# Attention and mixer on one core: f loaded by two broadcast transfers, one weight load on ScalarE's queue, the Exp table loaded early, new opening orders

## The chip, the cores and the metric

The kernel runs on one core of a Trainium2 chip. The metric is the device time of one execution in microseconds. Of three timed executions of the kernel before, the median is 926.94 us (926.46 to 927.48). One further execution was profiled; it took 927.18 us, and its span, from the first to the last instruction, is 925.4 us. Two kernels of this program count as different when their times differ by more than 0.2%, some 1.85 us.

## The reference

```python
# attention: 8 batches, 8 heads, 576 positions, head size 64; f is [8, 8, 576]
scores = scale * np.matmul(q, k.transpose(0, 1, 3, 2))
log_f = np.log(np.clip(f, 0.0001, 1.0))
cum = np.cumsum(log_f, axis=-1)
decay = cum[:, :, :, None] - cum[:, :, None, :]
scores = np.where(causal, -1000000000.0, scores + decay)
attn = np.exp(scores - max); attn = attn / (sum + 1e-09)
out = np.matmul(attn, v)
# mixer on x [8, 576, 512]
h = np.maximum(xt @ w_tok1, 0.0) @ w_tok2
u = x + h.transpose(0, 2, 1)
h2 = np.maximum(u @ w_ch1, 0.0) @ w_ch2
return u + h2
```

The four weight matrices arrive as 64-bit floats, two 32-bit words each, and the kernel decodes them itself.

## The kernel before

**Opening.** The 64 rows of f (one row per batch and head, 576 values of 4 bytes) are laid twice into a tile `xt` by four transfers of 32 rows, two on SP's queue and two on ScalarE's (`ld` in `decay`, L517). VectorE clips (L525), ScalarE takes the logarithm (L526), VectorE sums along the row (L528) and makes `cd` (L531, L533), ScalarE writes a copy times -8 (L536), and two transfers store that to DRAM as `decd` (L538), from where each pair of heads reads its decay `cb` (L732).

**Pairs of heads.** There are 32 pairs (n0, n1, ...). For each one `raw` holds q and k (L719), `vr` holds v. TensorE makes scores into eight banks (L747), for some pairs, n0 among them, it adds the decay by matmuls with `cd` (L774), for the others VectorE adds `cb`. VectorE reduces the minimum and frees the bank (L788), ScalarE takes the exponential (L792), TensorE transposes (L862), ScalarE or VectorE copy that out (L872, L870), TensorE multiplies by v (L891). While TensorE has nothing to do at the start, 36 small filling matmuls of the identity run (L545).

**Decoding.** `decode` loads a block of weights into one of three buffers `d_raw` (L559), and ScalarE (L572), VectorE (L576, L580, L584, L592) and GpSimd (L588, L492, L495) turn it into two 32-bit parts. The first five blocks belong to w_tok1; the first is loaded by two transfers, the second by one of 256 KB.

**Mixer.** After every four pairs the token mixer of half a batch runs; from about 380 us on the channel mixer of the whole output runs, nearly all of it matmuls.

**What sets the order.** `ORDER` is a table of numbers with one list for each engine and one for SP's queue: the operations in the order in which that engine issues them. Each engine issues strictly in that order, so an instruction that waits holds back all that stand behind it. For SP's queue there is also a pace: a transfer is issued only when an older one has landed, so that no more than about 1.2 MB stand between the two (`AHEAD`).

Of the kernel before, what the change touches and what calls it, by code (L numbers as in the profile page):

```python
# [67 lines left out]
    ),  # L68
    DVE=(
# [369 lines left out]
def build(nc, env, dims):  # L439
# [39 lines left out]
    def at(b):  # L479
        return env[b.kind][b.slot]  # L480
# [28 lines left out]
    def decay():  # L509
# [6 lines left out]
        def ld(eng, q):  # L516
            return eng.dma_start(at(w)[32 * q : 32 * q + 32, 0, :], fs[q // 2])  # L517

        p.op("POOL", 600, lambda: nc.gpsimd.memset(row(2), 0.0), wr=["zero"], bufs=[w, *HOLD.values()])
        for q in (0, 2):  # L520
            dma(lambda q=q: ld(nc.sync, q), 73728, wr=[("f", q)], bufs=[w])
# [1015 lines left out]
```

## Time and profile before

| | before |
|---|---|
| median of three runs | 926.94 us |
| profiled execution | 927.18 us, span 925.4 us |
| PE (TensorE) busy | 905.5 us, 98% |
| DVE (VectorE) busy | 710.2 us, 77% |
| ACT (ScalarE) busy | 520.6 us, 56% |
| POOL (GpSimd) busy | 237.2 us, 26% |
| DMA | 242.49 MB, mean 262 GB/s |

PE is the engine with the largest share, over the whole span. The shares are means over stages that differ: the first 20 us hold the opening, up to 380 us the pairs of heads and the token mixer run, then the channel mixer. SP, the queue that issues nearly all transfers, has no busy time of its own in these shares.

### The profile page before, as it was taken

What the parts mean: (1) busy time and instruction counts of PE and PEld (TensorE: products, weight loads), DVE (VectorE), ACT (ScalarE), POOL (GpSimd) and SP (SyncE); (2) the same over time, 40 slices, a digit from 0 to 9 for tenths busy, and PEclk for the clock granted to TensorE, in tenths of its full rate; (3) what the DMA queues carried; (4) which work ended last, traced back from release to release, by engine and by line L of the source; (5) the groups of instructions that cost most, each with busy time, mean ns of one, the idle gap of its engine ahead of it and who ended that gap; (6) DMA issues with size and microseconds to landing.
All of it is one profiled execution on the core that took longest, in us unless ns stands there. A gap on an engine that the chain in (4) does not pass through costs nothing.

```text
span 925.4 us, 26760 instructions
## 1 busy us (share of the span) xinstructions
PE 905.5 (98%) x10270; PEld 781.3 (84%) x10270; DVE 710.2 (77%) x1894; ACT 520.6 (56%) x1340; POOL 237.2 (26%) x320
## 2 busy tenths in 40 slices
PE   7999999999998999999999999999999999999998
PEld 5688888788887787888888888888888899999998
DVE  7998988888777777754699646986389955995497
ACT  5989998998788988731354123541135412542142
POOL 4577776766665562110000000000000000000000
PEclk9999999999999999999999999999999999999999
DMA  7999999998999698558887878888888799889986
GB/s 237 273 268 281 312 280 292 302 282 274 276 304 285 207 271 224 167 176 293 263 257 234 265 208 245 250 252 261 261 244 247 239 294 303 286 273 298 294 286 220
DMA packets 143871, 242.49 MB, mean 262 GB/s; under 512 B 15936, under 2 KB 71488, under 8 KB 143744
## 3 DMA queue, kind: packets, MB, share of 16 engines
q1 hardware_dynamic: 143648, 240.64, 84.8%
q8 instruction: 81, 1.33, 0.6%
q14 instruction: 46, 0.38, 0.1%
q10 hardware_dynamic: 96, 0.15, 0.0%
HBM read 199.52 MB, written 41.21 MB: 260 GB/s over the span
## 4 chain that ended last, share of the span: by engine, by line
PE 59%; DVE 2%; DMA 2%; POOL 1%; issue 0%; ACT 0%; SPq 0%; DVEq 0%; POOLq 0%
PE bank L1047 9%; PE bank L1049 9%; PE bank L1048 9%; PE bank L1128 9%; PE bank L1130 9%; PE bank L1129 9%; PE bank L1245 2%; DMA d_raw<-ud 1%; DVE pr L788 1%; PE bank L891 1%; PE bank L862 0%; DMA wq<-wd 0%; DMA recd<-rs 0%; POOL sg L495 0%; PE bank L747 0%
## 5 line engine op out<-in xcount | busy, mean ns | idle before, releaser
L792 ACT ACTIVATE pr<-pr,nmin 64x64 f32<-64x64 f32 (+4 forms) x320 | 176.7, 560 | 16.6 <-DVE nmin L788 16.2
L489 ACT ACTIVATE st<-H 128x512 fp32r<-128x512 f32 (+1 forms) x210 | 119.6, 586 | 89.0 <-PE bank L1129 63.3
L1128 PE MATMUL bank<-st,wq 128*128 128x512 f32 (+1 forms) x420 | 154.2, 367 | 0.3 <-DMA wq<-wd 0.3
L1130 PE MATMUL bank<-st,wq 128*128 128x512 f32 (+1 forms) x420 | 154.3, 367 | 0.0
L1129 PE MATMUL bank<-st,wq 128*128 128x512 f32 (+1 forms) x420 | 154.2, 367 | 0.0
L788 DVE CUSTOM_DVE_ANT_0 pr<-bank,cb 128x448 f32<-128x448 f32 (+3 forms) x260 | 108.7, 454 | 6.0 <-PE bank L747 1.8
L747 PE MATMUL bank<-raw 64*64 64x448 f32 (+6 forms) x1408 | 109.5, 397 | 2.6 <-DMA raw<-in_qk 1.3
L498 DVE TENSOR_TENSOR st<-H,st 128x512 fp32r<-128x512 f32 (+1 forms) x150 | 92.4, 631 | 14.6 <-ACT st L489 14.2
L891 PE MATMUL bank<-pf,vr 64*64 64x256 f32 (+3 forms) x2048 | 98.7, 317 | 1.5 <-ACT pf L872 0.5
L983 DVE TENSOR_TENSOR tmp<-bank,tmp 128x512 f32<-128x512 f32 (+1 forms) x80 | 50.2, 632 | 55.6 <-PE bank L1049 42.4
L872 ACT ACTIVATE pf<-bank 128x512 f32<-128x512 f32 x152 | 84.4, 596 | 11.2 <-PE bank L862 5.7
L1128 PEld LDWEIGHTS bank<-st,wq 128*128 128x128 f32 x420 | 78.8, 188 | 10.2 <-issue 0.6
L1130 PEld LDWEIGHTS bank<-st,wq 128*128 128x128 f32 x420 | 78.8, 188 | 9.9
L1129 PEld LDWEIGHTS bank<-st,wq 128*128 128x128 f32 x420 | 78.8, 188 | 9.6
L891 PEld LDWEIGHTS bank<-pf,vr 64*64 64x64 f32 x2048 | 76.4, 134 | 10.0 <-issue 2.0
L747 PEld LDWEIGHTS bank<-raw 64*64 64x64 f32 x1408 | 52.0, 132 | 27.7 <-issue 10.2
L1073 ACT ACTIVATE H<-bank 128x512 f32<-128x512 f32 (+1 forms) x30 | 16.5, 554 | 103.2 <-PE bank L1049 103.1
L1059 ACT ACTIVATE tmp<-bank 128x512 f32<-128x512 f32 (+1 forms) x30 | 16.6, 552 | 101.1 <-PE bank L1049 101.1
L862 PE MATMUL bank<-ident,pr 64*128 64x64 f32 x1536 | 65.0, 225 | 5.4 <-issue 2.1
L862 PEld LDWEIGHTS bank<-ident,pr 64*128 64x128 f32 x1536 | 58.8, 139 | 11.2 <-issue 5.0
L922 POOL TENSOR_TENSOR xt<-xt,rb 128x64 f32<-128x64 f32 (+1 forms) x64 | 52.5, 840 | 49.7 <-DVE xt L910 19.6
L792 ACT ACTIVATION_READ_ACCUMULATOR pr<-pr,nmin 128x1 f32 (+1 forms) x320 | 63.2, 198 | 0.0
(171 smaller groups left out, 2109.9 us busy)
## 6 DMA issues: line engine op xcount, KB each, us to landing
wq<-wd SPq DMA_DIRECT2D x420, 256.0 KB
raw<-in_qk SPq DMA_DIRECT2D x32, 576.0 KB
cb<-decd SPq DMA_DIRECT2D x26, 576.0 KB
d_raw<-in_w_ch SPq DMA_DIRECT2D x48, 256.0 KB
wd<-sg SPq DMA_DIRECT2D x24, 512.0 KB
vr<-in_v SPq DMA_DIRECT2D x64, 160.0 KB
rb<-recd SPq DMA_DIRECT2D x32, 320.0 KB
wd<-sg SPq DMA_DIRECT2D x24, 384.0 KB
```

The lines of the kernel that those rows point to most:

```text
L489: nc.scalar.activation(out, in_, func, scale=scale)
L498: nc.vector.tensor_tensor(out, in_, asf(hi), op=ALU.subtract)
L747: nc.tensor.matmul(at(buf)[HALF[h], of : of + n], q[:, i0 : i0 + D], k[:, j0 : j0 + n], start=t not in (0, 1), stop=not nd, skip_group_che ...
L788: nc.vector.tensor_tensor_reduce(o, x, y, -1.0 / D**0.5, c0[:m, NS + z : NS + z + 1] if t == 5 else 3e38, op0=ALU.add, op1=ALU.min, accum_ ...
L792: nc.scalar.activation(x, x, AF.Exp, bias=E["nmin"][sm][:m, t : t + 1], scale=-1.0, accum_out=E["rec"][rm][:m, c : c + 1])
L862: nc.tensor.transpose(at(ps[s])[:, k * D : (k + 1) * D], at(pr)[r, x, :, :].rearrange("p a b -> p (a b)"), E["ident"][r, r])
L872: p.op("ACT", d_act(512), lambda src_=src_, o=o: nc.scalar.activation(o(), src_(), AF.Copy), rd=[ps[s]], wr=[(pt, s)], bufs=[ps[s], pt])
L891: nc.tensor.matmul(at(av[z])[o, 256 - w : 256], at(vr)[r, vblk(j), :], at(pt)[r, c : c + w], start=j == 4, stop=gi == 2, skip_group_check= ...
L1047: nc.tensor.matmul(o, wt[:, 0, :], h_, start=(first and k == 0), stop=False, skip_group_check=True)
L1128: nc.tensor.matmul(o, wt[:, 0, :], h_, start=(first and x == 0), stop=False, skip_group_check=True)
L1129: nc.tensor.matmul(o, wt[:, 1, :], h_, start=False, stop=False, skip_group_check=True)
L1130: nc.tensor.matmul(o, wt[:, 0, :], l_, start=False, stop=(x == FX - 1), skip_group_check=True)
```

## The change

f comes by two transfers of 64 rows, one on each queue, each of which reads its 32 rows of f twice through a source that is broadcast over a leading count of two. The transfer of the second decoding's weights moves from SP's queue to ScalarE's, where it stands behind the first table load. A one-column Exp is put ahead of the copy times -8, so that the Exp table is loaded there and not at the first exponential. The orders of all engines are new in the opening and the first batches; from about the tenth pair of heads on they are the old ones, with numbers that are lower by two.

```diff
-        "14:12 145 135 146 136 26:2 139 155 28:3 156 140 185 31:11 193 202 42:3 188 45:4 165 49 168 171 267 275 218 284 "
...
+        "12:21 143 137 144 133 33 134 153 34:3 138 37:2 183 154 39 186 191 40 200 41:3 163 44:2 166 169 46 265 47 273 "
...
-        def ld(eng, q):
-            return eng.dma_start(at(w)[32 * q : 32 * q + 32, 0, :], fs[q // 2])
+        def ld(eng, s):
+            return eng.dma_start(at(w)[D * s : D * s + D, 0, :], fs[s : s + 1].to_broadcast([2, HB // 2, S]))
+
+        def neg():
+            nc.scalar.activation(E["lnx"], E["lnx"], AF.Exp)
+            return nc.scalar.activation(row(0), row(1), AF.Copy, scale=-8.0)
...
-        for q in (0, 2):
-            dma(lambda q=q: ld(nc.sync, q), 73728, wr=[("f", q)], bufs=[w])
-        for q in (1, 3):
-            p.op("ACT", 450, lambda q=q: ld(nc.scalar, q), wr=[("f", q)], bufs=[w], lat=2300, at=-1.0)
+        dma(lambda: ld(nc.sync, 0), 147456, wr=[("f", 0)], bufs=[w])
+        p.op("ACT", 450, lambda: ld(nc.scalar, 1), wr=[("f", 1)], bufs=[w], lat=2300, at=-1.0)
...
-        p.op("ACT", d_act(S, False), lambda: nc.scalar.activation(row(0), row(1), AF.Copy, scale=-8.0), rd=["c"], wr=["f"], bufs=[w])
+        p.op("ACT", d_act(S, False), neg, rd=["c"], wr=["f"], bufs=[w])
...
-            return nc.sync.dma_start(o, src.bitcast(U32).rearrange("... (n two) -> ... n two", two=2))
+            return (nc.scalar if tok == ("t1", 1) else nc.sync).dma_start(o, src.bitcast(U32).rearrange("... (n two) -> ... n two", two=2))
...
-            dma(lambda x=x: ld(*x), nb / len(loads), wr=[(rb, i)], bufs=[rb])
+            if tok == ("t1", 1):
+                p.op("ACT", 450, lambda x=x: ld(*x), wr=[(rb, i)], bufs=[rb], lat=4000, at=-1.0)
+            else:
+                dma(lambda x=x: ld(*x), nb / len(loads), wr=[(rb, i)], bufs=[rb])
```

SP's queue from its first transfer on, before (raw_183 is q and k of n0, raw_184 of n1; d_raw_150 holds the first decoding's weights, d_raw_151 the second's):

```order
L517 DMA xt_144<-in_f 32x576 x2
L719 DMA raw_183<-in_qk 128x1152
L559 DMA d_raw_150<-in_w_tok 64x512 x2
L559 DMA d_raw_151<-in_w_tok 128x512
L719 DMA raw_184<-in_qk 128x1152
L559 DMA d_raw_152<-in_w_tok 128x512
L538 DMA decd<-xt_144 32x576 x2
```

The same stretch of the change:

```order
L516 DMA xt_144<-in_f 64x1x576
L723 DMA raw_183<-in_qk 128x1152
L560 DMA d_raw_150<-in_w_tok 64x512 x2
L723 DMA raw_184<-in_qk 128x1152
L560 DMA d_raw_152<-in_w_tok 128x512
L539 DMA decd<-xt_144 32x576 x2
```

One transfer of f stands ahead of n0's q and k where two stood, and the second decoding's weights are gone from the queue.

ScalarE's instructions from its first transfer on, before:

```order
L517 DMA xt_144<-in_f 32x576 x2
L524 ACT_TABLE_LOAD
L524 ACTIVATE lnx<-rec_95 128x1
L526 ACTIVATE xt_144<-xt_144 128x576
L536 ACTIVATE xt_144<-xt_144 128x576
L572 ACTIVATE d_g_153<-d_raw_150 128x256
L572 ACTIVATE d_g_154<-d_raw_151 128x256
L572 ACTIVATE d_g_153<-d_raw_152 128x256
L792 ACT_TABLE_LOAD
L792 ACTIVATE pr_193,rec_92<-pr_193,nmin_89 64x64
```

The same stretch of the change:

```order
L516 DMA xt_144<-in_f 64x1x576
L525 ACT_TABLE_LOAD
L525 ACTIVATE lnx<-rec_95 128x1
L560 DMA d_raw_151<-in_w_tok 128x512
L527 ACTIVATE xt_144<-xt_144 128x576
L519 ACT_TABLE_LOAD
L519 ACTIVATE lnx<-lnx 128x1
L520 ACTIVATE xt_144<-xt_144 128x576
L576 ACTIVATE d_g_153<-d_raw_150 128x256
L576 ACTIVATE d_g_154<-d_raw_151 128x256
L576 ACTIVATE d_g_153<-d_raw_152 128x256
L796 ACTIVATE pr_193,rec_92<-pr_193,nmin_89 128x7x64
```

The second table load has moved from ahead of the first exponential to behind the logarithm, and a transfer stands between the first one-column activation and the logarithm.

VectorE's instructions from the clip on (idb and tri are small constants), before:

```order
L525 TENSOR_SCALAR xt_144<-xt_144 128x576
L1399 TENSOR_SCALAR idb<-ident 64x64 x2
L1400 TENSOR_SCALAR tri<-mask 64x64 x2
L528 SCALAR_TENSOR_TENSOR xt_144<-xt_144 128x576
L531 TENSOR_SCALAR cd<-xt_144 128x576
L533 SCALAR_TENSOR_TENSOR cd<-cd,lows,xt_144 128x576
L576 TENSOR_SCALAR d_g_153<-d_g_153 128x256
L580 TENSOR_SCALAR d_g_153<-d_g_153 128x256
L584 SCALAR_TENSOR_TENSOR d_g_153<-d_raw_150,d_g_153 128x256
L576 TENSOR_SCALAR d_g_154<-d_g_154 128x256
L788 ISA pr_193,nmin_89<-bank_64,mask 64x64
```

The same stretch of the change:

```order
L526 TENSOR_SCALAR xt_144<-xt_144 128x576
L1403 TENSOR_SCALAR idb<-ident 64x64 x2
L1404 TENSOR_SCALAR tri<-mask 64x64 x2
L529 SCALAR_TENSOR_TENSOR xt_144<-xt_144 128x576
L532 TENSOR_SCALAR cd<-xt_144 128x576
L534 SCALAR_TENSOR_TENSOR cd<-cd,lows,xt_144 128x576
L580 TENSOR_SCALAR d_g_153<-d_g_153 128x256
L584 TENSOR_SCALAR d_g_153<-d_g_153 128x256
L580 TENSOR_SCALAR d_g_154<-d_g_154 128x256
L588 SCALAR_TENSOR_TENSOR d_g_153<-d_raw_150,d_g_153 128x256
L584 TENSOR_SCALAR d_g_154<-d_g_154 128x256
L792 ISA pr_193,nmin_88<-bank_63,mask 128x7x64
```

All that works on f still stands ahead of the decoding and of the first reduction; one more decoding instruction now stands ahead of that reduction, which is another one. On TensorE, 21 filling matmuls stand ahead of n0's first scores where 12 stood.

## Rows read from the trace of the kernel before

**Rows 1.** Busy time of each engine by stage; last three columns: clock, DMA share, GB/s.
```profile
core 0: us, PE busy (x) PEld busy (x) DVE busy (x) ACT busy (x) POOL busy (x), PEclk, DMA share, GB/s
8.00:20.00 12.00, 11.09 (x164) 7.09 (x164) 10.38 (x44) 7.52 (x22) 6.12 (x10) 1.00 0.79 250
20.00:40.00 20.00, 17.46 (x367) 12.54 (x367) 20.00 (x86) 18.69 (x60) 9.81 (x15) 1.00 0.88 262
40.00:70.00 30.00, 28.92 (x580) 23.80 (x580) 28.62 (x100) 26.61 (x77) 22.59 (x29) 1.00 0.98 279
70.00:160.00 90.00, 89.76 (x1873) 77.09 (x1864) 79.29 (x293) 81.21 (x245) 67.16 (x88) 1.00 0.95 289
```

**Rows 2.** Timeline of the opening: start, us, engine, line, what, [idle before <-releaser].
```profile
0.74 0.87 SPq L517 DMA_DIRECT2D xt<-in_f  x2
...
3.94 0.46 DVE L525 TENSOR_SCALAR xt<-xt 128x576 f32<-128x576 f32 x1 [2.41 <-DMA xt<-in_f]
...
4.22 2.50 PE L545 MATMUL bank<-ident 128*64 128x48 f32 x22
...
7.10 0.82 DVE L533 SCALAR_TENSOR_TENSOR cd<-cd,lows,xt 128x576 fp32r<-128x576 f32 x1
...
8.00 1.85 PE L747 MATMUL bank<-raw 64*64 64x448 f32 x20 [1.28 <-DMA raw<-in_qk]
...
8.57 0.79 SPq L538 DMA_DIRECT2D decd<-xt  x2
...
8.97 0.80 ACT L572 ACTIVATE d_g<-d_raw 128x256 f32<-128x256 f32 x2 [1.68 <-DMA d_raw<-in_w_tok]
...
9.43 0.29 DVE L576 TENSOR_SCALAR d_g<-d_g 128x256 uint32<-128x256 uint32 x1 [1.51 <-ACT d_g L572]
...
10.09 0.43 DVE L584 SCALAR_TENSOR_TENSOR d_g<-d_raw,d_g 128x256 f32<-128x256 uint32 x1
...
13.71 1.28 ACT L792 ACT_TABLE_LOAD   x1
...
15.00 0.35 ACT L792 ACTIVATE pr<-pr,nmin 64x64 f32<-64x64 f32 x1
```

**Rows 3.** DMA view of the window 1.75 to 3.25 us: packets, MB, share.
```profile
DMA packets 210, 0.38 MB, mean 252 GB/s; under 512 B 64, under 2 KB 64, under 8 KB 210
...
q10 hardware_dynamic: 96, 0.15, 27.0%
```

**Rows 4.** DMA view of the whole span: packets, queue, issues by form with KB each.
```profile
DMA packets 143871, 242.49 MB, mean 262 GB/s; under 512 B 15936, under 2 KB 71488, under 8 KB 143744
...
q1 hardware_dynamic: 143648, 240.64, 84.8%
...
wq<-wd SPq DMA_DIRECT2D x420, 256.0 KB
...
recd<-rs SPq DMA_DIRECT2D x32, 5.0 KB
...
d_raw<-ud SPq DMA_DIRECT2D x4, 32.0 KB
xt<-ud SPq DMA_DIRECT2D x4, 32.0 KB
...
```

**Rows 5.** Three short windows around the transfers of f; columns as in Rows 1.
```profile
1.50:1.75 0.25, 0.00 (x0) 0.00 (x0) 0.03 (x1) 0.09 (x1) 0.25 (x2) 1.00 0.00 0
1.75:3.25 1.50, 1.41 (x4) 0.79 (x4) 0.00 (x0) 1.40 (x2) 1.14 (x7) 1.00 1.00 252
8.00:10.00 2.00, 2.00 (x22) 0.85 (x24) 0.53 (x2) 0.80 (x2) 0.00 (x0) 1.00 0.94 335
```

**Rows 6.** Timeline of TensorE near 289 us, after its longest idle stretch past the opening.
```profile
289.29 0.89 PE L862 MATMUL bank<-ident,pr 64*128 64x64 f32 x19 [2.12 <-issue]
```

**Rows 7.** The two windows that follow it; columns as in Rows 1.
```profile
290.00:292.00 2.00, 2.00 (x38) 1.88 (x38) 0.79 (x2) 2.00 (x5) 2.00 (x3) 0.50 0.65 222
292.00:294.00 2.00, 2.00 (x50) 1.91 (x46) 1.29 (x2) 2.00 (x8) 1.20 (x2) 0.70 1.04 339
```

More of the change, by code (lines that the diff above doesn't have):

```diff
@@ L514, in row @@
             return at(w)[:, i, :]
-        def ld(eng, q):
-            return eng.dma_start(at(w)[32 * q : 32 * q + 32, 0, :], fs[q // 2])
+        def ld(eng, s):
[3 more added lines that the diff above has]
+            return nc.scalar.activation(row(0), row(1), AF.Copy, scale=-8.0)
         p.op("POOL", 600, lambda: nc.gpsimd.memset(row(2), 0.0), wr=["zero"], bufs=[w, *HOLD.values()])
-        for q in (0, 2):
-            dma(lambda q=q: ld(nc.sync, q), 73728, wr=[("f", q)], bufs=[w])
-        for q in (1, 3):
-            p.op("ACT", 450, lambda q=q: ld(nc.scalar, q), wr=[("f", q)], bufs=[w], lat=2300, at=-1.0)
+        dma(lambda: ld(nc.sync, 0), 147456, wr=[("f", 0)], bufs=[w])
+        p.op("ACT", 450, lambda: ld(nc.scalar, 1), wr=[("f", 1)], bufs=[w], lat=2300, at=-1.0)
         p.op("ACT", 1500, lambda: nc.scalar.activation(E["lnx"], E["rec"][3][:, :1], AF.Ln), wr=["ln"], at=-1.0)
-        p.op("DVE", d_dve(S, True), lambda: nc.vector.tensor_scalar(row(0), row(0), 1e-4, 1.0, op0=ALU.max, op1=ALU.min), rd=[("f", q) for q in range(4)], wr=["f"], bufs=[w], port=True)
+        p.op("DVE", d_dve(S, True), lambda: nc.vector.tensor_scalar(row(0), row(0), 1e-4, 1.0, op0=ALU.max, op1=ALU.min), rd=[("f", q) for q in range(2)], wr=["f"], bufs=[w], port=True)
         p.op("ACT", d_act(S, False), lambda: nc.scalar.activation(row(0), row(0), AF.Ln), rd=["ln"], wr=["f"], bufs=[w])
```

397 rows, old and new, of tables (ACT, DVE, PE, POOL) are left out of this document.

## The prediction

> **What bounds the kernel now.** I read the stages first. From 20 to 40 us VectorE has no idle time at all (20.00 of 20.00 us) while TensorE lacks 2.5 us; from 40 to 70 both are nearly full; from 70 to 160 TensorE works 89.76 of 90 us and VectorE 79 [rows 1]. So the opening is VectorE's, and what VectorE loses there TensorE has lost when its own full stretch begins: nothing later gives it back. The question is then when VectorE becomes busy for good. The timeline says 9.43 us [rows 2]: the 1.51 us of idle time ahead of that end with ScalarE's first decoding step, which itself waited 1.68 us for the first decoding's weights, until 8.97. Ahead of it VectorE worked on f: the clip starts at 3.94, when f has landed, and cd is done at 7.10 + 0.82 = 7.92. f is thus 9.43 - 7.92 = 1.5 us early now, and no more. TensorE's first scores start at 8.00, when n0's q and k land; they aren't what VectorE waits for, since it has decoding to do until 10.6.
>
> The profiled execution takes 927.18 us for a span of 925.4; it lies 0.24 us above the median, and I forecast the median.
>
> **Two transfers of f, not four.** What goes away is one issue on SP and one on ScalarE, 0.87 / 2 = 0.43 us each [rows 2]. The bytes stay: 64 rows of 2304 bytes, twice, 295 kB. What may change is how many of the 16 DMA engines carry them. In the window in which f moves, 64 packets are under 512 bytes, and no row of f is that small: 16 for each of the four transfers. ScalarE's queue shows 96 packets for its two, and 96 = 2 x (32 rows + 16) [rows 3]. So a transfer ends with one small packet from each engine that it used, and a transfer of 32 rows used 16. It isn't always 16. The list holds 902 transfers on SP's queue (first line x420, the small ones x32, x4 and x4). With 16 small packets each these would be 14432; the 32 stores of `recd` add 32 x 20 rows of 256 bytes = 640, the eight 32 KB loads 8 x 128 = 1024 more, in all 16096. The page counts 15936 [rows 4]. With 10 engines for each `recd` store, whose outermost count is 20, the sum is 16096 - 32 x 6 = 15904, and 32 are left for the instruction queues. So the transfer is cut evenly along its outermost count: 32, 64 and 128 give 16, and 20 gives 10.
>
> The changed transfer writes 64 rows, but its source now begins with a count of two. If both sides have to be cut, it can only be cut in two. No row of before shows a transfer whose two sides differ in this way, so both ends stay open: 16 engines, or two. I take two, since a cut that only one side can follow is of no use to the other, and all other rows follow the outermost count.
>
> The Trainium skill says it outright (DMA: Bandwidth & Descriptors, Why a DMA increments its semaphore by 16 and not by 1): the engines used are the largest number up to 16 that divides the slowest dimension of both sides, and they are the lowest-numbered ones, so that both transfers of f would share the same two. The 32 stores with 10 engines agree with its first half. No run here shows the second yet.
>
> The cost. On two engines, the same two for both queues (that is assumed; separate pairs are a rival), each engine carries 295 / 2 = 147.5 kB. Over the whole span a busy engine moves 240.64 MB / (0.848 x 16 x 925.4 us) = 19.2 kB per us [rows 4]. While f moves it is 252 / 16 = 15.8, and from 8 to 10 us 335 / (0.94 x 16) = 22.3 [rows 5]. So f takes 7.7 us (6.6 to 9.3). Nothing moves ahead of 1.75 us, all small packets are through by 3.25, and the clip starts 0.69 later [rows 2, 3, 5]. f lands at 1.75 + 7.7 + 0.69 = 10.1 (9.0 to 11.8), not at 3.94. Clip to cd takes 7.92 - 3.94 = 3.98, and all of it stands ahead of the decoding in VectorE's order, so decoding starts at 14.1 (13.0 to 15.8) in place of 9.43. That is **+4.7 us** (+3.6 to +6.3).
>
> What is late next: q and k of n0 and the first weights stand behind f on these two engines. Their shares there are 590 / 16 = 36.9 and 262 / 16 = 16.4 kB, with the second weights 16.4 more, together 217 kB: 1.75 + 11.3 + 0.69 = 13.7, still ahead of 14.1. But the same arithmetic for before gives 1.75 + 71.7 / 19.2 + 0.69 = 6.2, and the weights came at 8.97, so up to 2.8 more, 16.5, and with 0.46 for ScalarE's step VectorE would start at 17.0, +7.5. TensorE's filling matmuls, 21 now, end near 4.22 + 20 x 2.50 / 11 = 8.8; then it idles some 4 us. After a pause of 2.12 us its granted clock was 0.50 for 2 us, the lower level (1.2 GHz), and 0.70 over the next two [rows 6, 7]. At half pace the first scores cost up to 1.6 us more, and the decoding ahead of the first reduction, four steps of 0.29 and one of 0.43, hides part of that. I add **0.5 us** (0 to 1.6) for both.
>
> **The other parts.** The second weights' issue on ScalarE, about 0.45 us, ends before the logarithm can start, now as before. On their own queue these 262 kB can take turns with n0's q and k, which were ahead of them: at worst 16.4 / 19.2 = 0.85 us later for all that lands; at best SP's queue is 0.43 earlier. I take **0**, as f hides either. The table load of 1.28 us ahead of the first exponential at 15.00 goes; behind the logarithm it lies beside the scan on VectorE (about as long) and delays at most the store of `decd`, now at 8.57. The gain stays on ScalarE, while VectorE is the bound: **0**, at best -1.0 if TensorE's transposes were waiting on that exponential alone. If f had been on time, the cover of this load would be the same scan. The new orders issue the same operations, and VectorE has no idle time in 20 to 40 us to win back: **0**, -1 to +1 for TensorE's 1.1 us of gaps from 40 to 70.
>
> The sum: 927.18 + 4.7 + 0.5 = 932.4, as a median 932.1; I forecast **932.1 us**. Its own range goes from +2.6 (3.6 - 1.0) to +8.5 (7.5 + 1.0): 929.5 to 935.4.
>
> **The rivals.** (a) f runs on 16 engines, as now. Then f stays early, decoding starts when the first weights land, between 0.43 earlier and 0.85 later: 926.5 to 927.8, no change. For it: the tile side has 64 rows. Against it: the stores with 10. (b) Two engines for each transfer, but not the same two: 73.7 kB each, 3.8 us, f at 6.3, cd at 10.3, +0.8: 927.7, no change. It decides where f lands before some 5.5 us; later than that, each us counts in full. (c) f on 16 engines, and what ScalarE gains passes, or the pause of 2.12 us with its slow clock [rows 6, 7] (2.12 + 2 x 0.5 + 2 x 0.3 = 3.7 us in all) doesn't return, as it hangs on instants that any new order moves: from 923.2 up to the bound of a difference at 925.1, faster. Nothing in the rows says that it goes. (d) The second weights hold n0's q and k back beside a prompt f; this is the 0.85 of (a) and not slower by itself.
>
> The Trainium skill has a rule for (d) (DMA: Bandwidth & Descriptors, Queues, rings and completion order): each DMA engine takes turns between the queues that have work for it. By that rule the upper end of (a), 927.8, would be the likelier one; no row of before shows two full queues at once for long.
>
> **How the numbers follow.** Two engines and the same two: 0.74. Of that 0.03 ends within 0.2% (1.85 us), with the fastest rate and the gains of the other parts. (a) 0.14, (b) 0.05, (c) 0.07. So faster 0.07, within 0.2% 0.22, slower 0.71. Without (a) and (b) the range would hold 7 in 10 at most, so it takes them in: 926.4 to 935.4.
>
> **What would show it.** After the change the clip starts near 10 us, waiting for f, and VectorE idles until then; the DMA share between 2 and 8 us falls; ScalarE's queue shows 64 + 2 + 128 + 16 = 210 packets, against 224 on 16 engines; the first exponential comes near 19 to 20 us. The prediction is wrong if the clip starts near 4 us, and its size is wrong if f lands as here and VectorE's loss is then made up before 70 us, where the rows show no room for it.

## The result, and the profile after

The changed kernel takes 937.24 us (median of 6 runs, 933.97 to 939.86), the kernel before 926.75 us beside it: ratio 1.0109, with an interval of 1.0085 to 1.0133, so 7.9 to 12.3 us more. I had forecast 932.1, in a range up to 935.4. The profiled execution took 937.34 us for a span of 935.5.

First the opening, in the timeline of the changed kernel (start, length, engine, line, what, idle before it), as in [rows 2]:

```profile
0.74 1.13 ACTq L516 DMA_DIRECT2D xt<-in_f  x1
0.74 0.72 SPq L516 DMA_DIRECT2D xt<-in_f  x1
...
12.84 0.46 DVE L526 TENSOR_SCALAR xt<-xt 128x576 f32<-128x576 f32 x1 [11.31 <-DMA xt<-in_f]
...
14.18 2.41 PE L751 MATMUL bank<-raw 64*64 64x448 f32 x20 [6.80 <-DMA raw<-in_qk]
...
16.00 0.82 DVE L534 SCALAR_TENSOR_TENSOR cd<-cd,lows,xt 128x576 fp32r<-128x576 f32 x1
...
16.74 0.29 DVE L580 TENSOR_SCALAR d_g<-d_g 128x256 uint32<-128x256 uint32 x1
...
20.55 0.62 DVE L792 CUSTOM_DVE_ANT_0 pr<-bank,mask 128x448 f32<-128x448 f32 x1 [1.05 <-PE bank L778]
...
21.76 0.67 ACT L796 ACTIVATE pr<-pr,nmin 128x448 f32<-128x448 f32 x1 [0.72 <-DVE nmin L792]
```

The clip waits for f until 12.84 us, not 3.94. VectorE's decoding follows cd at 16.74, 7.3 us later than before, and ScalarE's first exponential comes at 21.76, not at 15.00. Then there is a wait that the kernel before did not have: VectorE's reduction at 20.55 waits for a bank that TensorE fills with the falling term (L778).

The windows answer to [rows 1], columns as there (the last three: granted clock, DMA share, GB/s):

```profile
8.00:20.00 12.00, 5.44 (x36) 2.36 (x36) 6.40 (x19) 3.48 (x6) 1.39 (x3) 0.54 0.43 117
20.00:40.00 20.00, 18.48 (x256) 11.72 (x256) 16.64 (x72) 14.85 (x49) 8.89 (x14) 0.76 0.69 232
40.00:70.00 30.00, 27.97 (x596) 22.03 (x595) 29.76 (x113) 26.18 (x79) 18.68 (x25) 1.00 0.87 270
70.00:160.00 90.00, 89.24 (x1854) 76.32 (x1846) 80.24 (x291) 82.04 (x245) 69.51 (x88) 1.00 0.95 286
10.00:12.00 2.00, 0.00 (x0) 0.00 (x0) 0.00 (x0) 0.00 (x0) 0.00 (x0) 0.50 0.13 49
```

VectorE is busy 6.40 us from 8 to 20 (10.38 before) and 16.64 of 20 after that, where it had no idle time before. In the last row no engine computes, and the DMA moves 49 GB/s. VectorE's waits in the first 45 us (total, times, longest):

```profile
DVE xt L526 <- DMA xt<-in_f: 11.3, 1, 11.3
DVE pr L792 <- PE bank L778: 3.6, 3, 1.4
```

The DMA view, of the window 1.75 to 3.25 us as in [rows 3], then of the whole span as in [rows 4]:

```profile
DMA packets 21, 0.07 MB, mean 49 GB/s; under 512 B 0, under 2 KB 0, under 8 KB 21
```
```profile
DMA packets 143811, 242.49 MB, mean 259 GB/s; under 512 B 15876, under 2 KB 71428, under 8 KB 143684
...
q10 hardware_dynamic: 210, 0.41, 0.2%
```

21 packets where 210 went before: a few engines work. ScalarE's queue counts 210 packets, and the small ones fall by 60, from 4 x 16 to 2 x 2.

How far the loss travels is seen from the 16 stores of `ud` on SP's queue (the token mixer's u of half a batch, each), the first, the tenth and the eleventh, of the kernel before and then of the changed one:

```profile
80.29 0.59 SPq L1331 DMA_DIRECT2D ud<-xt  x1
...
291.24 1.01 SPq L1331 DMA_DIRECT2D ud<-xt  x1
315.06 0.32 SPq L1331 DMA_DIRECT2D ud<-xt  x1
```
```profile
90.45 0.59 SPq L1335 DMA_DIRECT2D ud<-xt  x1
...
302.60 0.61 SPq L1335 DMA_DIRECT2D ud<-xt  x1
324.16 0.32 SPq L1335 DMA_DIRECT2D ud<-xt  x1
```

10.2 us are lost by the first store, of which 7.3 are the later start of the decoding, and 11.4 by the tenth; 2.3 come back by the eleventh; the span is 10.1 longer. TensorE's pause of 2.12 us near 289 us [rows 6] has no counterpart in the changed kernel. That the 2.3 are this pause is not shown: it lies ahead of the tenth store, and the return shows only behind it. So a loss as large as the whole one stands at the first store, but it is not simply carried from there to the end (more on this below).

### The profile page after: what moved, and what is told of

It reads as the page before. It is cut to its first block, busy times and chain, and to the rows that moved or that the text cites. A ratio compares the mean times of both kernels' runs of the same rounds, so it can differ in the third digit from the quotient of the medians.

```text
span 935.5 us, 26750 instructions
## 1 busy us (share of the span) xinstructions
PE 910.8 (97%) x10270; PEld 781.2 (84%) x10270; DVE 710.1 (76%) x1894; ACT 520.9 (56%) x1341; POOL 237.4 (25%) x320
## 4 chain that ended last, share of the span: by engine, by line
PE 77%; DVE 8%; DMA 6%; POOL 3%; issue 3%; ACT 1%; SPq 1%; DVEq 0%; POOLq 0%; ACTq 0%
PE bank L1051 9%; PE bank L1052 9%; PE bank L1053 9%; PE bank L1132 9%; PE bank L1133 9%; PE bank L1134 9%; PE bank L1249 7%; PE bank L751 5%; PE bank L895 5%; DVE pr L792 3%; PE bank L866 3%; DMA rb<-recd 1%; POOL xt L926 1%; DMA xt<-in_f 1%; DMA d_raw<-ud 1%
## 5 line engine op out<-in xcount | busy, mean ns | idle before, releaser
L751 PE MATMUL bank<-raw 64*64 64x448 f32 (+6 forms) x1408 | 115.8, 412 | 7.9 <-DMA raw<-in_qk 6.8
L895 PE MATMUL bank<-pf,vr 64*64 64x128 f32 (+3 forms) x2048 | 98.4, 314 | 2.8 <-issue 1.2
L876 ACT ACTIVATE pf<-bank 128x512 f32<-128x512 f32 x152 | 83.9, 597 | 11.8 <-PE bank L866 6.8
L1132 PEld LDWEIGHTS bank<-st,wq 128*128 128x128 f32 x420 | 78.8, 188 | 10.1 <-issue 0.5
L751 PEld LDWEIGHTS bank<-raw 64*64 64x64 f32 x1408 | 53.8, 137 | 35.6 <-issue 11.8
```

What stands on the lines that cost most here:

```text
L751: nc.tensor.matmul(at(buf)[HALF[h], of : of + n], q[:, i0 : i0 + D], k[:, j0 : j0 + n], start=t not in (0, 1), stop=not nd, skip_group_che ...
L895: nc.tensor.matmul(at(av[z])[o, 256 - w : 256], at(vr)[r, vblk(j), :], at(pt)[r, c : c + w], start=j == 4, stop=gi == 2, skip_group_check= ...
L1132: nc.tensor.matmul(o, wt[:, 0, :], h_, start=(first and x == 0), stop=False, skip_group_check=True)
```

## The experiments

The ratios are to the kernel before on the same chip, with their 95% interval; "us" behind one is the ratio applied to that kernel's median (925.0 to 926.3). Single executions of that kernel lie between 921.7 and 930.3 us, so a difference of 2 us is read from medians with their interval, and an instant in one profile only as what that execution did.

**f's form.** Four transfers again, all else as changed:

```diff
-            return eng.dma_start(at(w)[D * s : D * s + D, 0, :], fs[s : s + 1].to_broadcast([2, HB // 2, S]))
+            for q in (2 * s, 2 * s + 1):
+                o = eng.dma_start(at(w)[32 * q : 32 * q + 32, 0, :], fs[s])
+            return o
```

> The changed kernel with f in four transfers of 32 rows again; the second weights' queue, the table load and the new orders stay as changed. Theory A (the source that begins with a count of two is the whole loss, the other parts are worth nothing): the clip starts near 4 us, ScalarE's queue shows 64 + 32 + 128 + 16 = 240 packets, VectorE decodes from about 9.4, the granted clock stays 1.00 through the opening, and the time is 926.8 us (925.5 to 928). Rival B (the other parts carry what the forecast lacked, about 5 us): 929 to 932 us, with VectorE's decoding late although the clip is early. Rival C (the other parts gain, hidden by f): 923 to 925 us.

Measured: 1.0024 (1.0004 to 1.0043), +2.2 us. The clip starts at 3.82 us and ScalarE's queue counts 240 packets, so f's form is the main cause; but 2.2 stay, between A's 0 and B's 5. VectorE waits 1.2 and 0.6 us for banks and is busy 19.39 of the 20 us from 20 to 40.

Two transfers with another outermost count, 32 and then 4:

```diff
+  (32) fs[s].rearrange("i (o x) -> i o x", o=1).to_broadcast([HB // 2, 2, S])
+  (4)  fs[s][:4].rearrange("i (o x) -> i o x", o=1).to_broadcast([4, 16, S])
```

> The changed kernel, f still in two transfers of 64 rows and 147 kB, but the source begins with the 32 rows and repeats each row twice inside (rows stand in another order in the tile, so the falling term of the scores is that of other rows). Theory A (the outermost count decides the engines): 16 engines for each, ScalarE's queue shows 64 + 16 + 128 + 16 = 224 packets, the clip starts near 4 us, and the time is that of the four transfers, 926.8 us (925.5 to 928). Rival D (two large transfers or a source read twice are slow as such): the clip near 12.8 us and 937 us.

> The changed kernel, each of f's two transfers with a source that begins with a count of four (four rows, each repeated 16 times; other values, the same 147 kB). Theory A (the same lowest engines carry both, and the time goes with the bytes on one engine: 73.7 kB in place of 147.5 kB): ScalarE's queue shows 64 + 4 + 128 + 16 = 212 packets, the clip starts at 7.5 to 8.5 us, and the time is 930 to 933 us. Rival H (large transfers of f wait for something other than their engines): the clip stays near 12.8 us and the time at 936 to 937 us.

Measured: with 32, 224 packets and a ratio of 1.0012 (0.9992 to 1.0032); with 4, 212 packets and 1.0086 (1.0071 to 1.0101), +8.0 us, the upper end of A. The row of the clip, with 32 and then with 4:

```profile
4.35 0.46 DVE L526 TENSOR_SCALAR xt<-xt 128x576 f32<-128x576 f32 x1 [2.82 <-DMA xt<-in_f]
8.54 0.46 DVE L526 TENSOR_SCALAR xt<-xt 128x576 f32<-128x576 f32 x1 [7.01 <-DMA xt<-in_f]
```

Number and size of the transfers are the same in all three, so the outermost count decides: with 2, 4 and 32 the clip starts at 12.84, 8.54 and 4.35. Halving the bytes on one engine brings f 4.30 us earlier. The time gained is 2.1 us (10.1 to 8.0), though by the two intervals 4.30 is not excluded; in the profile with 4 VectorE waited 4.9 us for banks. That both transfers use the same engines, the changed kernel's own trace says, in the DMA view from 10 to 11 us (packets, MB, share of 16 engines):

```profile
q1 hardware_dynamic: 13, 0.03, 7.3%
q10 hardware_dynamic: 11, 0.02, 5.7%
```

Both queues are at work there, and together they keep 13.0% of 16, 2.1 engines, busy. By the packet list of the kept trace q1 then moves SP's rows of f (2304 bytes each, 5.43 to 12.26 us), while ScalarE's rows of f (2.22 to 9.53) are through. What q10 still moves are rows of the second weights, 2048 bytes each: 112 of the 128 were through by 7 us, and the last 16, the share of two engines, came only from 9.0 us on, behind ScalarE's f. So the engines that ScalarE's f held are the two that SP's f still holds.

The changed form in the kernel before, nothing else; run on two chips:

```diff
-            return eng.dma_start(at(w)[32 * q : 32 * q + 32, 0, :], fs[q // 2])
+            s = int(eng is nc.scalar)
+            if s not in sent:
+                sent[s] = eng.dma_start(at(w)[D * s : D * s + D, 0, :], fs[s : s + 1].to_broadcast([2, HB // 2, S]))
+            return sent[s]
```

> The kernel before with nothing but f's two transfers in the changed form (source beginning with a count of two); the second weights stay on SP's queue, the table load and the orders are old. Theory A: the clip near 12.8 us and the whole loss, 937 us (935.5 to 938.5). Rival B (part of the loss is the second weights' queue, the table load or the orders): f lands as forecast near 10 to 11 us and the time is 932 to 934 us.

> The old orders and parts with f in the changed form, once more on this chip: 931.5 to 932.5 us; TensorE at half pace in its first scores, but VectorE waits only 0.5 us for banks, since the old order puts the falling terms right behind one another.

Measured: 1.0066 (1.0042 to 1.0091), +6.1 us, and 1.0069 (1.0042 to 1.0095), +6.4. In the first profile the clip starts at 12.85 us, the decoding at 16.75, and the first `ud` store at 87.72, 7.4 later than before: the shift of the start, to 0.1 us. (In the second they are 12.68, 16.59 and 88.41.) A's 937 is wrong, and so is the reason that B gave: f lands as late as in the changed kernel, though the second weights are on SP's queue. VectorE waited 0.5 us for banks in the first of the two profiles and 1.5 in the second.

**The other parts.** The table load and the weights' queue with the old orders, then that with f's changed form:

```diff
+            nc.scalar.activation(E["lnx"], E["lnx"], AF.Exp)        # ahead of the scaling by -8
+            return (nc.scalar if tok == ("t1", 1) else nc.sync).dma_start(o, ...)
-        "2 1 132 51 50 60 181 69   (SP)   "3:3 7 11   (ACT)
+        "2 1 132 51 50 181 69      (SP)   "3:2 60 5 7 11   (ACT)
```

> The kernel before, its orders and its four transfers of f kept, with the table load behind the logarithm and the second weights on ScalarE's queue. Theory F (the 2.4 us that stayed with f prompt come from the new orders: TensorE now puts four 448-column scores and a filling matmul between the first and the second falling term, so VectorE's second reduction comes later): no loss, 925.5 us (924.5 to 926.5), VectorE busy 34 to 35 of the first 40 us. Rival G (they come from the second weights' queue or the table load): 927.5 to 929 us.

> As the run with old orders and new parts, with f in the two transfers of the change: the whole change without its orders. Theory F: as the broadcast form alone, 931.7 us (930 to 933), so that the orders carry the 4 us up to the changed kernel. Rival G: 934 to 937 us.

Measured: 1.0017 (1.0001 to 1.0033), +1.6 us, and 1.0092 (1.0073 to 1.0112), +8.5. Both medians lie between F and G, and their intervals reach into both, so neither is singled out. In the first, decoding starts at 9.40, as before, and yet VectorE waits 2.7 us for banks that TensorE fills; TensorE runs the first scores at half the pace there (below).

The orders alone, and each part alone:

> The new orders alone: four transfers of f, the table load where it was before, the second weights on SP's queue. Theory F: 928 us (927 to 929.5), VectorE busy some 33.4 of the first 40 us, as with all parts but f's form. Rival G: 925.5 us (924.5 to 926.5).

> The kernel before with the second weights issued by ScalarE, nothing else. Both new parts together gave +1.6 us with the old orders, and there TensorE ran the first scores at half pace (3.48 us in place of 1.85). Theory W (the queue is what costs: its packets take turns with n0's loads): 926.5 to 927 us, and n0's scores or the decoding start later than 8.0 and 9.43 us. Rival P (neither part costs; whether TensorE runs fast when n0's scores come is open in each execution): 925 to 926 us, with both starts as before.

> The kernel before with the exponential's table loaded behind the logarithm, nothing else. Theory W (the queue costs, the table is free): 925 us (924 to 926). Rival T (the table load costs, as it delays the first decoding step or decd's store): 926.5 to 927 us, with the first decoding step later than 8.97 us. Rival U (it gains, as I bounded it): 924 us.

Measured: the new orders with the old parts 1.0058 (1.0037 to 1.0079), +5.4 us, above F's range, into which the interval reaches. TensorE's first scores and VectorE's first reduction there:

```profile
8.66 2.41 PE L749 MATMUL bank<-raw 64*64 64x448 f32 x20
...
11.57 0.62 DVE L790 CUSTOM_DVE_ANT_0 pr<-bank,mask 128x448 f32<-128x448 f32 x1 [1.46 <-PE bank L776]
```

The weights' queue gave 1.0007 (0.9993 to 1.0021), with the decoding at 9.89, 0.46 later than before, as W has it; the table load 0.9996 (0.9979 to 1.0013), with the decoding at 9.07. Neither part is told from nothing. The orders cost by themselves: 5.4 us alone, 2.2 together with the parts.

**TensorE's pace.** All fills tripled; then also 14 matmuls between the first scores and the falling terms; then the same with only the early fills tripled (the diff). The fourth run is the changed kernel on the chip of the third, the last bridges the old orders with f's changed form:

```diff
-            "PE", [tp_(P, 64)], lambda: nc.tensor.matmul(...),
+            "PE", [tp_(P, 64)], lambda: [nc.tensor.matmul(...) for _ in range(3 if i < 21 else 1)][-1],
+            if n2 == 0 and ts == (5,):
+                for _ in range(14):
+                    nc.tensor.matmul(at(where[0][5][0])[:64, 448:496], E["ident"][:, :64], E["ident"][:, :48], start=True, stop=True)
```

> The changed kernel with each of the 40 filling matmuls issued three times, so that TensorE has work from about 4.2 to 13.6 us in place of 7.4. Theory A1 (TensorE's pause from 7.4 to 14.2 us is what brings the granted clock to 0.50 until about 28 us, and the half clock costs the 3.4 us that VectorE waits between 20 and 40 us): granted clock 1.00 from 10 to 30 us, no wait of VectorE for a bank there, 933.8 us (932.5 to 935). Rival E (the clock is lower there for another reason, or the waits come from the new orders): 937 us, with the clock still 0.50 or the waits still there.

> The changed kernel with the tripled filling matmuls and 14 more between the first scores and the falling terms, so that TensorE has hardly a pause from 4.2 us until cd is there at 16.8. With tripled fills alone the pause moved to 15.5 to 16.9 us, the granted clock fell to 0.57 behind it and the time stayed. Theory A1 (the half clock behind a pause costs the waits of VectorE for the first falling terms): granted clock 1.00 from 14 to 30 us, VectorE's waits for banks in the first 45 us under 1.5 us in place of 3.6, and 933.8 us (932.5 to 935.5). Rival E (the waits come from the order in which the new tables put scores, fills and falling terms): waits of 3 us or more at full clock, 936 to 937 us.

> The changed kernel with only the filling matmuls ahead of n0's scores tripled (not those in later gaps, which took up to 0.7 us more each) and 14 matmuls between the first scores and the falling terms. Theory A1 (the half pace behind TensorE's pause, in an order that puts four scores between the first falling terms, costs the waits of VectorE): granted clock 1.00 from 8 to 30 us, the waits for banks at most 1 us in place of 3.6, the first store of ud 2 to 3 us earlier than in the changed kernel, and 933.5 to 935 us. Rival E: the waits go and the time stays within 1 us of the changed kernel.

> The changed kernel unaltered, on the chip and in the rounds of the three that follow, so that differences of 2 us can be read. 936 to 937.5 us beside some 926 for the kernel before.

> The same with TensorE kept at work from 4.2 us to the falling terms (filling matmuls ahead of n0's scores six times, 9 more behind the scores of the last column block). Theory A1: as VectorE hardly waited for TensorE there, 0 to 1 us less, 931 to 932 us. Rival X (half pace costs the same 2 us in any order): 929.5 to 930.5 us.

Measured: 1.0110 (1.0081 to 1.0139) with the fills alone; 1.0099 (1.0077 to 1.0121) bridged, 935.4 us, at the upper edge of A1; 1.0124 (1.0091 to 1.0156) bridged cleanly, beside 1.0104 (1.0076 to 1.0132) for the changed kernel; 1.0079 (1.0051 to 1.0107) for the old orders bridged, beside 1.0069; that is 933.6 us, above both A1 and X. With the fills alone VectorE still waited 3.7 us for banks. The windows of the cleanly bridged run and, below, of the changed kernel beside it:

```profile
14.00:20.00 6.00, 5.45 (x72) 3.56 (x76) 5.72 (x16) 2.91 (x6) 1.31 (x3) 1.00 0.42 119
20.00:30.00 10.00, 8.32 (x140) 5.53 (x131) 9.61 (x47) 8.22 (x30) 6.01 (x10) 1.00 0.90 295
```
```profile
14.00:20.00 6.00, 5.04 (x34) 2.05 (x34) 5.66 (x17) 3.22 (x6) 1.08 (x2) 0.50 0.43 119
20.00:30.00 10.00, 8.97 (x124) 5.61 (x123) 8.09 (x39) 6.68 (x23) 5.33 (x9) 0.89 0.78 246
```

In the profiled execution the bridge does what it should: granted clock 1.00 (2.4 GHz) where it was 0.50 (1.2 GHz), no wait of VectorE for a bank left (2.5 us beside it), and the first `ud` store 2.3 us earlier, 0.3 of it because f landed earlier (12.93 against 13.24). In the first bridged run the waits were 1.1 us. So with the new orders the waits do come from the pace. But by the eleventh store the 2.3 us are gone; the first and the eleventh, bridged cleanly and, below, beside it:

```profile
87.41 0.59 SPq L1338 DMA_DIRECT2D ud<-xt  x1
...
321.33 0.32 SPq L1338 DMA_DIRECT2D ud<-xt  x1
```
```profile
89.67 0.59 SPq L1335 DMA_DIRECT2D ud<-xt  x1
...
321.32 0.32 SPq L1335 DMA_DIRECT2D ud<-xt  x1
```

The medians give no gain either, 936.37 against 935.15 us, near what E has. But the difference of the two ratios, 1.9 us, is uncertain by some 4, and the profiled execution was the fastest of the six (931.91; 934.76 for the one beside it) and the only one with a mean granted clock of 1.000; the others have 0.992 to 0.998 and go up to 941.28. Whether the bridge held in those is not known. So A1's price is not shown in the time, and not excluded.

Last, the kernel before with its first 8 fills doubled (`range(2 if i < 8 else 1)`):

> The kernel before with the first 8 filling matmuls issued twice (19 ahead of n0's scores in place of 11), so that TensorE has no pause between 6.7 and 8.0 us. Theory P (TensorE's pace in n0's scores decides some of the time): the scores run at full pace (1.3 to 1.9 us) and the time is 923.5 to 925 us, better than before. Rival V (VectorE is the bound there at either pace, or the extra matmuls run at half pace and push the scores to 8.7 us): 925 to 926.5 us.

Measured: 1.0009 (0.9998 to 1.0020). The scores start at 8.44 and take 2.86 us, where P has 1.3 to 1.9: the 19 filling matmuls take 4.29 us, half pace, and push the scores, as V has it. No run beats the kernel before.

## Why the prediction was wrong

**What bounds the kernel: right in the main, too strong as "nothing later gives it back".** The loss stands at the first `ud` store, 10.2 us, and 10.1 at the end; that the two agree is in part luck. In the second profile of the same kernel it is 9.4 at the first store, 6.3 at the eleventh and 7.5 at the end; with f's form alone 7.4, 3.3 (318.38 us) and 5.1, for a start 7.3 late. Rival (c), the pause that does not come again, can be part of this, but not of the 2.3 us that the bridge gained and lost again, as neither the bridged execution nor the one beside it has that pause. Three runs whose time is not told from the kernel before have their first store at 81.45 to 82.07, not 80.29.

**Two engines, the same two: right.** 210 packets, as named. The Trainium skill's rule (DMA: Bandwidth & Descriptors, Why a DMA increments its semaphore by 16 and not by 1) gives 2, 4, 16 and 16 engines for the outermost counts 2, 4, 32 and four transfers of 32 rows; by that rule ScalarE's queue counts 210, 212, 224 and 240, and the traces agree. That the two transfers share their engines, the 2.1 busy engines and the late rows of the second weights show; which numbers these have, no run does. One reading on the way was off: the 32 small packets that were left over are not the instruction queues' but 16 for each of ScalarE's two transfers of f, and with them the sum of 15936 is exact.

**"f lands at 1.75 + 7.7 + 0.69 = 10.1": the first step that failed, in its size.** It landed at 12.84, above my 11.8. The first packet of f comes between 2.0 and 2.5 us, not at 1.75, and 147.5 kB from about 2.2 to 12.84 - 0.69 make 14.8 kB per us and engine, where I took 19.2 and at least 15.8. From 10 to 12 us, when hardly any other engine has work, the DMA moves 49 GB/s, 24.5 kB per us for each of two. So they were slower while the others were full: by the packet list a row of f took 156 ns on the mean from 5.4 to 10 us and 96 behind it. A mean over a full span is no rate for two engines that share with 14 busy ones. From clip to cd it took 3.98, as forecast. The term of 4.7 us for the start measured 7.3, and f's form alone cost 6.1 and 6.4 us.

**"I add 0.5 us" for what is late next: not refuted by the times.** n0's q and k came at 14.18 (forecast 13.7). The half clock lasted from 9.0 to 29.5 us by the clock records of the trace (the windows give 0.54 and 0.76), not 2 us, and VectorE waited 3.6 us for banks; bridged, the waits went and the median time did not fall. What the half clock costs in time is open.

**"The other parts: 0, -1 to +1": the second step that failed.** With f prompt they cost 2.2 us (0.4 to 4.0). I asked what the new orders could win back where VectorE had no idle time, and not what they could lose. From 4.22 us on, the new orders have 20 filling matmuls ahead of n0's scores where 11 stood; in the run with the orders alone the scores start behind them at 8.66 us and run at half pace (2.41 us, against 1.32 in the bridged runs), and VectorE's first reduction waits 1.46 us for its falling term (1.25 with the new parts). That is not the whole cause: the kernel before with 19 of them has such a wait too (1.1 us) and costs 0.8 us (-0.2 to 1.9). Which rows of the orders cost the rest is open. The weights' queue delayed the decoding by 0.46, inside my bound of 0.85; its time is not told from nothing. Nor did an issue of 0.43 us go away on each queue: the one transfer of f takes 0.72 us to issue on SP and 1.13 on ScalarE, where two took 0.87 and 0.90.

The sum is 6.1 + 2.2 = 8.3 us, inside the interval of 7.9 to 12.3. Whether the 1.8 up to 10.1 are more than scatter is open. Of the signs, the 210 packets and VectorE's idling came; the clip was 2.7 us later than said, the first exponential at 21.76 and not near 19 to 20, and the DMA share from 2 to 8 us fell only from 0.98 to 0.90.

## What to carry to other kernels

A transfer is cut along the outermost count of both sides: if one merges two loads through a broadcast, the large count belongs outside and the broadcast inside, or a few engines carry everything (2 here, in place of 16). The rate of a narrow transfer is to be read where the other engines are busy, and bounded well below the mean. Where the engine that a new order serves has no idle time, the order can win nothing there and still lose, so its bounds are not even on both sides of zero. And an instant in one profile does not stand for the time: the first store moved by 0.7 to 0.8 us between two executions of the same kernel (87.72 and 88.41, 90.45 and 89.67), and what was lost by then was in part made up later.

## What the runs showed of the hardware

In the opening the clock column can say 1.00 while TensorE runs at half pace. The 20 matmuls of the first scores in the old order took 1.85 us before, 3.48 in the run with the broadcast alone, where the column says 0.50, and 3.48 in the run with the old orders and new parts; its timeline row and its window:

```profile
7.99 3.48 PE L754 MATMUL bank<-raw 64*64 64x448 f32 x20 [1.18 <-DMA raw<-in_qk]
```
```profile
8.00:20.00 12.00, 12.00 (x100) 6.88 (x104) 7.84 (x36) 4.49 (x15) 4.52 (x7) 1.00 0.68 209
```

So there the pace is to be read from the durations. The kept traces show why: the column is made from clock records, and ahead of the first one it stands at 1.00 with nothing read. The first record, at full level in all of these, begins at 17.48 us in the run with 3.48; at 6.50, 6.24 and 6.22 in the kernel before, with the weights' queue alone and with the table load alone, which show 1.85 each; and at 10.54 in the kernel before with 8 fills doubled, which shows 2.86 from 8.44 on. So the matmuls ran at half pace until the first record: in all of these the first 22 filling rows from 4.22 us on took 2.4 to 2.6 us (38 took 4.29 with the fills doubled), and in the kernel before 22 like them took 1.67 at 14.64 us. The run with 3.48 and the three with 1.85 have the same filling matmuls; what lets the full level come at 6.2 us in one and at 17.5 in another, no run shows. With 3.48 VectorE waited 2.7 us for banks, with 1.85 not at all.
